# The first layer norm of two row groups taken by features instead of by rows

## The chip, the cores and the metric

The kernel runs on one core of one Trainium2 chip. The metric is the device time of one execution in microseconds (us); it is given as the median of three runs. TensorE (PE) multiplies matrices into PSUM, VectorE (DVE), ScalarE (ACT) and GpSimd (POOL) work elementwise, and SyncE (SP) issues the transfers (DMA). Each engine runs its own instructions strictly in the order of the program, and waits where an operand is not there yet.

## What is computed

```
mod = silu(c) @ w_mod                  # six rows of 448: sa, ca, ga, sb, cb, gb
h = layernorm(x) * (1 + ca) + sa       # x: 2048 rows of 448 features, f32
x = x + ga * attention(h)              # q, k, v from h @ wqkv; 16 heads of 28
h = layernorm(x) * (1 + cb) + sb
x = x + gb * gated_mlp(h)              # gelu, a 2048 x 2048 mix over the rows, a gate
```

`layernorm` takes from each row its mean and divides by the square root of its variance plus 1e-5. The change is in the first of the two norms.

## The kernel before

**Groups and layout.** The 2048 rows are four groups g of 512, each of four tiles of 128 rows. The norm needs mean and variance of a row, so x is loaded with rows on partitions (`load_x`, L179). But the matmuls that follow sum over the features, and so want h turned: `hT[g]` has features on partitions, in four blocks c of 128 (the last one has 64 features, held twice), and 512 rows along the free dimension. Each matrix is split in a high part (rounded to the fast f32r format) and a low part (the rest), and `STEPS` (L27) lists the 11 pairs of parts that are multiplied for one result. The parts of `hT[g]` are read in the order high 0, high 2, high 0, high 2, low 0, low 2, high 1, high 1, low 1, and last block 3 (high and low in one).

**The norm of a group.** `ln_stat` (L276) takes mean and variance of a tile on DVE (bn_stats and bn_aggr); `ln_rs` and `rstd_of` (L99) make the reciprocal root on POOL; `ln_norm` (L288) subtracts and scales on DVE (`xn`, L292), and ACT repeats 64 columns (L300). `ln_transpose` (L104) turns the four tiles with 16 transposes on PE (`tp`, L111) into four PSUM banks; for each block ACT applies 1 + ca and sa (L118, `hfull`) and rounds to the high part (L125), and DVE takes the low part (`sub`, L82). `ln_next(g)` (L542) does that for group g, and the statistics and `ln_norm` of group g + 1 between.

**The order around it.** The schedule is written out by hand; program order is the order on every engine. The loop `for g in range(1, NG)` (L562) has for g = 1 and 2: `v_tile(4g)`, `v_tile(4g + 1)`, `ln_next(g + 1)`, `v_tile(4g + 2)`, `v_tile(4g + 3)`, then two `qk_unit` of group g; for g = 3 two `qk_unit` come first. `v_tile` (L323) is 11 matmuls (`pv`, L317) and a copy by ACT; `qk_unit` (L329) is 11 matmuls (`pq`, L335), the split by ACT (L348) and DVE, and two stores to memory by SP (L354). PSUM has seven banks that go round (`bank`, L161).

**What is woven in.** `load_mod` (L167) loads columns of w_mod, `mod_acc` (L228) sums them on DVE, `mod_split` (L245) splits the sum: the high part (`acc_h`) by ACT, the low part (`acc_l`) by the engine that it is given, POOL for pair 1. `mod_sum` (L256) adds over partitions with two matmuls for each of two parts (`pc`, L260), and `mod_bc` and `mod_col` take the results. For g = 2 the split of pair 1 stands in `ln_next(3)`, and its `mod_sum` behind `v_tile(11)`.

**Transfers.** SP issues nearly all of them, in program order, and they run through one queue. A transfer that waits for its data holds up the ones behind it.

Of the kernel before, what the change touches and what calls it, by code (L numbers as in the profile page):

```python
# [20 lines left out]
NG = 4  # L21
# [9 lines left out]


@with_exitstack
def tile_adaln_mha_gmlp(ctx, tc, x, wqkv, wo, w_in, w_spT, b_sp, w_out, cT, w_mod0, w_mod, out):
    nc = tc.nc
    ctx.enter_context(tc.manual_schedule())
    pe, dve, act, pool, sp = nc.tensor, nc.vector, nc.scalar, nc.gpsimd, nc.sync
# [61 lines left out]
    def rstd_of(var, rs, n):  # L99

        pool.tensor_scalar(out=rs, in0=var, scalar1=EPS, scalar2=None, op0=ALU.add)
        pool.tensor_tensor(out=rs, in0=rs, in1=mhalf[:, :n], op=ALU.pow)

    def ln_transpose(xns, full_pool, dsts, scol, bcol, engs, los=(pool,) * 4, mid=None, after=None):  # L104

        tps = []
        for c in range(4):
            tp = bank("tp")
            tps.append(tp)
            for t in range(4):  # L110
                pe.transpose(tp[:, t * 128 : (t + 1) * 128], xns[t][:, c * 128 : (c + 1) * 128], ident)  # L111
        if mid:
            mid()
        for c in (0, 2, 1, 3):
            tp = tps[c]
            f = full_pool.tile([128, 512], F32, name="hfull")
            if engs[c] is act:
                act.activation(f, tp, AF.Identity, scale=scol[:, c : c + 1], bias=bcol[:, c : c + 1])  # L118
            else:
                engs[c].tensor_scalar(  # L120
                    out=f, in0=tp, scalar1=scol[:, c : c + 1], scalar2=bcol[:, c : c + 1], op0=ALU.mult, op1=ALU.add
                )
            hi = dsts[:, c if c < 3 else 6, :]
            if engs[c] is act:
                act.activation(hi, f, AF.Copy)  # L125
            else:
                engs[c].tensor_copy(hi, f)
            if c < 3:
                sub(los[c], dsts[:, 3 + c, :], f, hi)
            else:  # L130
                sub(los[c], hi[64:128], f[64:128], hi[64:128])
            if after:
                after(c)
# [33 lines left out]
    def load_mod(pair, eng):  # L167
        for k in range(4):
            wms[pair, k] = e1.tile([128, 2 * D], F32, name="wm", tag=("wm", "wm", "raw")[pair], bufs=4)[:, : 2 * D if k < 3 else D]
            c0 = ((pair - 1) * 7 + 2 * k) * D * 128  # L170
            eng.dma_start(wms[pair, k], w_mod[c0 : c0 + (2 if k < 3 else 1) * D * 128].rearrange("(r n) -> r n", r=128))
# [7 lines left out]
    def load_x(g, eng):  # L179
        xg = e1.tile([128, 4, D], F32, name="xg")  # L180
        for t0, t1 in ((0, 1), (1, 2), (2, 4)) if g == 0 else ((0, 4),):
            (act if t1 - t0 == 1 else eng).dma_start(xg[:, t0:t1, :], x[g, :, t0:t1])
        for t in range(4):
            xts[4 * g + t] = xg[:, t, :]
# [43 lines left out]
    def mod_acc(pair, k):  # L228
        if k == 0:
            accs[pair] = e2.tile([128, 2, D], F32, name="acc")  # L230
        wm, acc = wms.pop((pair, k)), accs[pair]
        if k < 3:
            wm = wm.rearrange("r (p n) -> r p n", p=2)
        if k == 0:
            dve.tensor_scalar(out=acc, in0=wm, scalar1=silu[:, 0:1], scalar2=None, op0=ALU.mult)
        elif k < 3:
            dve.scalar_tensor_tensor(out=acc, in0=wm, scalar=silu[:, k : k + 1], in1=acc, op0=ALU.mult, op1=ALU.add)
        else:
            half_rows(wm, [acc[:, part] for part in range(2)])
# [5 lines left out]
    def mod_split(pair, eng, pool_l, tag_l, bufs_l):  # L245

        acc = accs.pop(pair)
        accs[pair] = []
        for part in range(2):
            h = stage.tile([128, 512], F32R, name="acc_h", tag="qf")[:, :D]  # L250
            l = pool_l.tile([128, D], F32R, name="acc_l", tag=tag_l, bufs=bufs_l)
            act.activation(h, acc[:, part, :], AF.Copy)
            sub(eng, l, acc[:, part, :], h)
            accs[pair].append((h, l))
# [21 lines left out]
    def ln_stat(g, ts):  # L276
        if g not in mv1:
            mv1[g] = e1.tile([128, 4, 2], F32, name="mv"), e1.tile([128, 4], F32, name="rs")
        for t in ts:
            st = e1.tile([128, 6], F32, name="st", bufs=4)  # L280
            dve.bn_stats(out=st, in_=xts[4 * g + t])
            dve.bn_aggr(out=mv1[g][0][:, t, :], in_=st)

    def ln_rs(g, a, e):
        mv, rs = mv1[g]
        rstd_of(mv[:, a:e, 1], rs[:, a:e], e - a)

    def ln_norm(g, ts):  # L288
        mv, rs = mv1[g]
        for t in ts:  # L290
            xn = e1.tile([128, 512], F32, name="xn", bufs=4)
            dve.tensor_scalar(  # L292
                out=xn[:, :D],
                in0=xts.pop(4 * g + t),
                scalar1=mv[:, t, 0:1],
                scalar2=rs[:, t : t + 1],
                op0=ALU.subtract,
                op1=ALU.mult,
            )
            act.activation(xn[:, D:], xn[:, 384:D], AF.Copy)  # L300
            xn1.setdefault(g, []).append(xn)
# [21 lines left out]
    def v_tile(kt):  # L323
        v_copy(*v_mm(kt))
# [206 lines left out]
    qk_lo("a", 1, dve)  # L531
    qk_lo("a", 3, dve)
    load_mod(1, sp)
    ln_norm(1, range(4))
    qk_unit((0, 3), 0, order=HI_FIRST)

    def ln_step(g, t):
        ln_stat(g, (t,))
        if t % 2:
            ln_rs(g, t - 1, t + 1)  # L540

    def ln_next(g):  # L542

        if g + 1 < NG:
            ln_transpose(
                xn1.pop(g), e1, hT[g], cols["ca"], cols["sa"], (act,) * 4, (dve,) * 4, None,
                lambda c: ln_step(g + 1, (0, 2, 1, 3).index(c)),
            )
            ln_norm(g + 1, range(4))
        else:  # L550
            ln_transpose(
                xn1.pop(g), e1, hT[g], cols["ca"], cols["sa"], (act,) * 4, (dve,) * 4, None, lambda c: c == 2 and mod_split(1, pool, e1, "wm", 4)
            )

    ln_next(1)
    load_x(3, sp)
    qk_unit((1,), 0)
    qk_unit((2,), 0)
# [3 lines left out]
    for g in range(1, NG):  # L562
        if g == 3:
            early.close()
            stk = att.enter_context(tc.tile_pool(name="stk", bufs=1))
            kq = [[stk.tile([128, S], F32R, name=f"{n}st{i}") for n in "kq"] for i in range(3)]
            kst, qst = [a[0] for a in kq], [a[1] for a in kq]
            npool = att.enter_context(tc.tile_pool(name="npool", bufs=2))
            late_s = ExitStack()
            late_l = late_s.enter_context(tc.tile_pool(name="late_l", bufs=2))  # L570

            def pads(i, eng):

                dve.memset(kst[i][64:128, :].bitcast(F32), 0.0)
                eng.memset(qst[i][64:128, :].bitcast(F32), 0.0)
                pool.memset(kst[i][64:86, :].bitcast(F32), 1.0)

            pads(0, dve)

            def load_head(h, c0=0, c1=S):  # L580
                k, q = kst[h % 3], qst[h % 3]
                if h > 2:
                    sp.dma_start(q[84:86, :].bitcast(F32), q[86:88, :].bitcast(F32))
                for r0, i in ((0, 0), (56, 1), (28, 0)):
                    sp.dma_start(k[r0 : r0 + 28, c0:c1].bitcast(F32), qk_scr[i][D + h * DH : D + (h + 1) * DH, c0:c1])
                for r0, i in ((0, 0), (28, 1), (56, 0)):
                    sp.dma_start(q[r0 : r0 + 28, c0:c1].bitcast(F32), qk_scr[i][h * DH : (h + 1) * DH, c0:c1])

            load_head(0, 0, 1536)
            for m in (0, 3):  # L590
                qk_unit((m,), g)
            load_head(0, 1536, S)
        v_tile(4 * g)
        if g == 3:
            mod_split(2, dve, late_l, "acc_l", 2)
        v_tile(4 * g + 1)
        if g == 3:
            pads(1, pool)
            pads(2, pool)
        if g + 1 < NG:  # L600
            ln_next(g + 1)
        for k in range(2):
            v_tile(4 * g + 2 + k)
            if g == 2 and k == 1:
                mod_bc("ga", 1, 0)
                mod_col("sb", 1, 1, 0.0)
            if g == 1 or g == 2 and k == 1:
                mod_acc(g, k if g == 1 else 0)
        if g < 3:
            for k, m in enumerate((0, 3)):  # L610
                qk_unit((m,), g)
                mod_acc(g, 3 - g + k)
            if g == 2:
                mod_acc(g, 3)
# [887 lines left out]
```

## Time and profile before

| | |
|---|---|
| median of three runs | 1394.73 us (1394.36 to 1395.47) |
| the profiled execution, its own time | 1395.17 us |
| its span, first to last instruction | 1393.4 us |
| instructions | 20303 |
| granted clock of TensorE, mean | 1.000 |
| busy: PE, DVE, ACT, POOL | 1388.3, 1024.4, 779.9, 286.2 us |

The profile is that of one execution. Its views used here are the page (busy times, the chain that ended last), the timeline of one engine (start, length, engine, line, operation, output<-inputs, count, and in brackets the idle time before it and what ended it), the groups by line (busy time and mean in ns, then the idle time before them), the view of one tile or line (shortest, median and longest duration in ns), and the table by stretches (busy time of each engine with the number of instructions, granted clock, DMA share, GB/s). All times are from the start of the span. PE matmuls overlap, so the distance from one start to the next is what one costs.

### The profile page before, as it was taken

The numbers are of one execution on the slowest core, as the hardware profiler recorded it, in microseconds if no ns is written. First come the engines' busy times: TensorE is split into PE (matmuls) and PEld (weight loads), VectorE is DVE, ScalarE is ACT, GpSimd is POOL, SyncE is SP. The second block draws the span as 40 slices with busy tenths as digits, with TensorE's granted clock in tenths as the row PEclk, the third lists the DMA queues.
The fourth block names the chain that finished last, engine by engine and source line by source line (L and its number), as shares of the span: only waits on it lengthen the run. The fifth ranks groups of instructions, "written<-read, shape, count | busy, mean of one in ns | idle before, by whom it ended". The sixth has DMA issues, their size and how long they took to land.

```text
span 1393.4 us, 20303 instructions
## 1 busy us (share of the span) xinstructions
PE 1388.3 (100%) x7170; PEld 988.5 (71%) x7170; DVE 1024.4 (74%) x1742; ACT 779.9 (56%) x1498; POOL 286.2 (21%) x306
## 2 busy tenths in 40 slices
PE   9999999999999999999999999999999999999998
PEld 8888655555555555555555555988998888888888
DVE  7798888888888888888888851850366655668574
ACT  6623677766666777777777779363234544434211
POOL 2144212221224243323200021000142430000000
PEclk9999999999999999999999999999999999999999
DMA  8464644655465556555323002434103333445453
GB/s 285 143 177 173 188 115 151 176 169 156 152 174 162 166 163 185 165 160 155 108 68 78 20 18 72 165 119 140 46 9 105 112 111 110 143 138 164 142 171 113
DMA packets 99489, 187.01 MB, mean 134 GB/s; under 512 B 17656, under 2 KB 29434, under 8 KB 96842
## 3 DMA queue, kind: packets, MB, share of 16 engines
q1 hardware_dynamic: 96670, 181.42, 43.0%
q10 hardware_dynamic: 2718, 4.30, 0.8%
q8 instruction: 56, 0.92, 0.3%
q14 instruction: 45, 0.37, 0.1%
HBM read 130.42 MB, written 50.46 MB: 130 GB/s over the span
## 4 chain that ended last, share of the span: by engine, by line
PE 98%; DMA 1%; DVE 0%; SPq 0%; POOL 0%; issue 0%; ACT 0%
PE st_ps L671 19%; PE o_ps L686 17%; PE mt L639 17%; PE acc L1246 7%; PE acc L1247 7%; PE acc L1248 7%; PE z_ps L1172 5%; PE z_ps L1058 5%; PE pq L335 5%; PE wo_ps L927 3%; PE pv L317 2%; PE y_ps L1353 2%; PE y_ps L1352 2%; PE y_ps L1354 2%; PE tp L111 1%; DMA xg<-in_x_dram 1%
## 5 line engine op out<-in xcount | busy, mean ns | idle before, releaser
L644 DVE TENSOR_REDUCE pm<-mt 128x1 f32<-128x512 f32 x1024 | 631.0, 682 | 85.9 <-PE mt L639 85.8
L675 ACT ACTIVATE P<-st_ps 128x512 f32<-128x512 f32 x1024 | 514.6, 632 | 201.7 <-PE st_ps L671 201.7
L671 PE MATMUL st_ps<-qst,kst 128*128 128x512 f32 x1024 | 404.4, 406 | 0.0
L639 PE MATMUL mt<-kst,qst 128*128 128x512 f32 x1024 | 402.4, 393 | 0.0
L671 PEld LDWEIGHTS st_ps<-qst,kst 128*128 128x128 f32 x1024 | 191.2, 187 | 141.1 <-issue 93.1
L686 PE MATMUL o_ps<-P,V 128*32 128x512 f32 x2048 | 247.1, 598 | 0.0
L639 PEld LDWEIGHTS mt<-kst,qst 128*128 128x128 f32 x1024 | 192.4, 188 | 31.8
L790 POOL TENSOR_TENSOR ws_raw<-ws_raw 128x512 f32<-128x512 f32 x80 | 103.1, 1289 | 293.5 <-DMA ws_raw<-in_w_spT_dram 293.4
L1134 ACT ACTIVATE wsp_h<-raw_sp 128x512 fp32r<-128x512 f32 x112 | 69.9, 631 | 153.5 <-PE acc L1248 104.0
L686 PEld LDWEIGHTS o_ps<-P,V 128*32 128x32 f32 x2048 | 54.6, 109 | 122.9 <-issue 114.6
L82 DVE TENSOR_TENSOR wsp_l<-raw_sp,wsp_h 128x512 fp32r<-128x512 f32 x112 | 80.6, 729 | 82.1 <-ACT wsp_h L1134 81.4
L1246 PE MATMUL acc<-wsp_h,heapA 128*128 128x512 f32 x224 | 87.3, 390 | 0.0
L1247 PE MATMUL acc<-wsp_l,heapA 128*128 128x512 f32 x224 | 87.2, 389 | 0.0
L1248 PE MATMUL acc<-wsp_h,heapA 128*128 128x512 f32 x224 | 87.2, 389 | 0.0
L1247 PE MATMUL acc<-wsp_l,heapB 128*128 128x512 f32 x174 | 67.7, 389 | 0.0
L1248 PE MATMUL acc<-wsp_h,heapB 128*128 128x512 f32 x174 | 67.7, 389 | 0.0
L1246 PE MATMUL acc<-wsp_h,heapB 128*128 128x512 f32 x174 | 67.7, 389 | 0.0
L335 PE MATMUL pq<-heapD,heapD 128*128 128x512 f32 x196 | 61.9, 390 | 0.0
L1176 DVE BATCH_NORM_STATS2 stz<-z 128x6 f32<-128x448 f32 x32 | 19.9, 625 | 50.4 <-ACT z L1175 29.8
L1246 PEld LDWEIGHTS acc<-wsp_h,heapA 128*128 128x128 f32 x224 | 42.1, 188 | 9.0 <-DVE cD L1252 0.3
L1248 PEld LDWEIGHTS acc<-wsp_h,heapA 128*128 128x128 f32 x224 | 42.0, 188 | 8.7
L1247 PEld LDWEIGHTS acc<-wsp_l,heapA 128*128 128x128 f32 x224 | 42.1, 188 | 8.5
(225 smaller groups left out, 1597.5 us busy)
## 6 DMA issues: line engine op xcount, KB each, us to landing
ws_raw<-in_w_spT_dram SPq DMA_DIRECT2D x160, 256.0 KB
ws_scr<-ws_raw SPq DMA_DIRECT2D x80, 256.0 KB
raw_sp<-ws_scr SPq DMA_DIRECT2D x80, 256.0 KB
kst<-qk_scr SPq DMA_DIRECT2D x45, 224.0 KB
qst<-qk_scr SPq DMA_DIRECT2D x45, 224.0 KB
raw_sp<-in_w_spT_dram SPq DMA_DIRECT2D x32, 256.0 KB
qk_scr<-qh SPq DMA_DIRECT2D x28, 256.0 KB
qk_scr<-ql SPq DMA_DIRECT2D x28, 256.0 KB
```

The source lines that it names most:

```text
L82: eng.tensor_tensor(out=dst, in0=a, in1=hi.bitcast(F32), op=ALU.subtract)
L335: pe.matmul(pq, wqk[:, b, m * 128 : (m + 1) * 128], hT[g][:, a, :], start=j == 0, stop=j == NST - 1)
L639: pe.matmul(mt, qst[h % 3][:, t * 128 : (t + 1) * 128], kst[h % 3][:, kb * 512 : (kb + 1) * 512], start=True, stop=True)
L644: dve.tensor_reduce(out=pms[h][:, t, kb : kb + 1], in_=mt, axis=AX.X, op=ALU.max)
L671: pe.matmul(st, kst[h % 3][:, kt * 128 : (kt + 1) * 128], qst[h % 3][:, qb * 512 : (qb + 1) * 512], start=True, stop=True)
L675: act.activation(p, st, AF.Exp, scale=SCALE)
L686: pe.matmul(otile[h][32 * qb : 32 * qb + 32, :], V[:, kt, h, :], ptiles.pop((u, qb)), start=kt == 0, stop=kt == NT - 1)
L790: pool.tensor_tensor(out=a, in0=a, in1=b, op=SUMS[i // 16][2])
L1134: act.activation(hi, raw, AF.Copy)
L1246: pe.matmul(acc[i], zh, hi, start=st == 0, stop=False)
L1247: pe.matmul(acc[i], zh, lo, start=False, stop=False)
L1248: pe.matmul(acc[i], zl, hi, start=False, stop=st == 7)
```

## The change

Groups 0 and 1 stay. For groups 2 and 3, x is also laid out turned in memory (`xT`: per group four blocks of 128 features by 512 rows, the last one's 64 features twice), and is loaded in that form (`load_xT`). The statistics are taken from x with rows on partitions as before. `ln_rows` makes of them, per row, the factor (reciprocal root) and the addend (minus mean times root), stores both as two lines of 512 in memory, each as 512 single elements, and loads each line back onto all 128 partitions (`abr`). `ln_rank` multiplies a block by the one and adds the other, in place, two tensor_tensor on DVE or POOL; `ln_fin` does the rest (1 + ca and sa on ACT, high part on ACT, low part on DVE). The transposes, `xn` and the PSUM banks of these groups are gone. Group 3's rows are loaded (`load_x(3)`) after the stores and loads of group 2's two lines.

```diff
+    ln_stat(2, (0,))
     ln_norm(1, range(4))
     qk_unit((0, 3), 0, order=HI_FIRST)
...
+    def load_xT(g):
+        for c in (0, 2, 1, 3):
+            xcs[g, c] = e1.tile([128, 512], F32, name="xc", tag="xn", bufs=4)
+            sp.dma_start(xcs[g, c], xT[g - 2, c])
+
+    def ln_rows(g):
+
+        mv, rs = mv1[g]
+        rstd_of(mv[:, :, 1], rs, 4)
+        ab = e1.tile([128, 2, 4], F32, name="ab")
+        pool.tensor_copy(ab[:, 0, :], rs)
+        dve.scalar_tensor_tensor(out=ab[:, 1, :], in0=mv[:, :, 0], scalar=-1.0, in1=rs, op0=ALU.mult, op1=ALU.mult)
+        dst = scr.tile([2, 512], F32, name=f"ab_scr{g}")
+        for i in range(2):
+            sp.dma_start(dst[i].rearrange("(t p) -> p t", p=128), ab[:, i, :])
+        abs_[g] = []
+        for i in range(2):
+            t = e1.tile([128, 512], F32, name="abr", tag="hfull")
+            sp.dma_start(t, dst[i].rearrange("(o n) -> o n", o=1).broadcast_to([128, 512]))
+            abs_[g].append(t)
+
+    def ln_rank(g, c, eng):
+        for t, op in zip(abs_[g], (ALU.mult, ALU.add)):
+            eng.tensor_tensor(out=xcs[g, c], in0=xcs[g, c], in1=t, op=op)
+
+    def ln_fin(g, c):
+        xc, hi = xcs.pop((g, c)), hT[g][:, c if c < 3 else 6, :]
+        act.activation(xc, xc, AF.Identity, scale=cols["ca"][:, c : c + 1], bias=cols["sa"][:, c : c + 1])
+        act.activation(hi, xc, AF.Copy)
+        if c < 3:
+            sub(dve, hT[g][:, 3 + c, :], xc, hi)
+        else:
+            sub(dve, hi[64:128], xc[64:128], hi[64:128])
 
     def ln_next(g):
 
-        if g + 1 < NG:
-            ln_transpose(
-                xn1.pop(g), e1, hT[g], cols["ca"], cols["sa"], (act,) * 4, (dve,) * 4, None,
-                lambda c: ln_step(g + 1, (0, 2, 1, 3).index(c)),
-            )
-            ln_norm(g + 1, range(4))
-        else:
-            ln_transpose(
-                xn1.pop(g), e1, hT[g], cols["ca"], cols["sa"], (act,) * 4, (dve,) * 4, None, lambda c: c == 2 and mod_split(1, pool, e1, "wm", 4)
-            )
+        ln_transpose(
+            xn1.pop(g), e1, hT[g], cols["ca"], cols["sa"], (act,) * 4, (dve,) * 4, None,
+            lambda c: c != 3 and ln_stat(2, ((0, 2, 1).index(c) + 1,)),
+        )
 
     ln_next(1)
+    load_xT(2)
+    ln_rows(2)
     load_x(3, sp)
...
-        if g + 1 < NG:
-            ln_next(g + 1)
-        for k in range(2):
-            v_tile(4 * g + 2 + k)
-            if g == 2 and k == 1:
+        if g < 3:
+            for c, eng in ((0, dve), (1, dve), (2, pool), (3, pool)) if g == 1 else ((1, dve), (0, pool), (2, pool), (3, pool)):
+                ln_rank(g + 1, c, eng)
+        if g == 1:
+            ln_fin(2, 0)
+            ln_stat(3, (0, 1))
+            v_tile(6)
+            ln_fin(2, 1)
+            ln_stat(3, (2,))
+            mod_acc(1, 0)
+            v_tile(7)
+            ln_fin(2, 2)
+            ln_stat(3, (3,))
+            ln_fin(2, 3)
+            load_xT(3)
+            ln_rows(3)
+            mod_acc(1, 1)
+        else:
+            v_tile(4 * g + 2)
+            if g == 2:
+                ln_fin(3, 1)
+                mod_split(1, pool, e1, "wm", 4)
+            v_tile(4 * g + 3)
+            if g == 2:
+                ln_fin(3, 0)
                 mod_bc("ga", 1, 0)
                 mod_col("sb", 1, 1, 0.0)
-            if g == 1 or g == 2 and k == 1:
-                mod_acc(g, k if g == 1 else 0)
+                mod_acc(2, 0)
         if g < 3:
             for k, m in enumerate((0, 3)):
                 qk_unit((m,), g)
+                if g == 2:
+                    ln_fin(3, 2 + k)
                 mod_acc(g, 3 - g + k)
```

More of the change, by code (lines that the diff above doesn't have):

```diff
@@ L33, in tile_adaln_mha_gmlp @@
 @with_exitstack
-def tile_adaln_mha_gmlp(ctx, tc, x, wqkv, wo, w_in, w_spT, b_sp, w_out, cT, w_mod0, w_mod, out):
+def tile_adaln_mha_gmlp(ctx, tc, x, xT, wqkv, wo, w_in, w_spT, b_sp, w_out, cT, w_mod0, w_mod, out):
     nc = tc.nc
@@ L533, in tile_adaln_mha_gmlp @@
     load_mod(1, sp)
+    ln_stat(2, (0,))
     ln_norm(1, range(4))
     qk_unit((0, 3), 0, order=HI_FIRST)
[L537 to L540, printed above, removed]
-    def ln_next(g):
-        if g + 1 < NG:
-            ln_transpose(
-                xn1.pop(g), e1, hT[g], cols["ca"], cols["sa"], (act,) * 4, (dve,) * 4, None,
-                lambda c: ln_step(g + 1, (0, 2, 1, 3).index(c)),
-            )
-            ln_norm(g + 1, range(4))
-        else:
-            ln_transpose(
-                xn1.pop(g), e1, hT[g], cols["ca"], cols["sa"], (act,) * 4, (dve,) * 4, None, lambda c: c == 2 and mod_split(1, pool, e1, "wm", 4)
-            )
+    xcs, abs_ = {}, {}
@@ L1462 @@
     cT[:64, 3] = cT[64:, 4] = _np.asarray(inputs["c"]).reshape(448)[384:]
+    xt = _np.asarray(inputs["A_x"])[0].T
     wm = _np.asarray(inputs["w_mod"]).reshape(448, 3, 2, 448)
@@ L1479 @@
         "x": _np.asarray(inputs["A_x"])[0].reshape(4, 4, 128, 448).transpose(0, 2, 1, 3),
+        "xT": _np.stack([xt[:128], xt[128:256], xt[256:384], _np.concatenate([xt[384:], xt[384:]])])
+        .reshape(4, 128, 4, 512)
+        .transpose(2, 0, 1, 3)[2:],
         "wqkv": twice(inputs["A_wqkv"]),
```

## The prediction, made before the changed kernel was run

> **What bounds the kernel now.** I read the page's busy table and its chain first, then TensorE's own chain for the stretch the change touches (30 to 75 us), then each other engine's timeline there.
>
> ```profile
> PE 1388.3 (100%) x7170; PEld 988.5 (71%) x7170; DVE 1024.4 (74%) x1742; ACT 779.9 (56%) x1498; POOL 286.2 (21%) x306
> PE 98%; DMA 1%; DVE 0%; SPq 0%; POOL 0%; issue 0%; ACT 0%
> ```
>
> TensorE (PE) is the bound: it is busy throughout and is 98% of the chain. So removed PE time is gained in full, and any wait put on PE is lost in full. The chain of the stretch, in order of time (start, length, what):
>
> ```profile
> 30.26 5.01 PE pq L335 x22
> 35.27 4.48 PE pv L317 x22
> 39.76 1.75 PE tp L111 x16
> 41.51 4.69 PE pv L317 x22
> 46.19 5.04 PE pq L335 x22
> 51.23 4.48 PE pv L317 x22
> 55.71 1.75 PE tp L111 x16
> 57.46 4.49 PE pv L317 x22
> 61.95 0.81 PE pc L260 x4
> 62.76 9.99 PE pq L335 x44
> ```
>
> No gap: `v_tile` (pv) costs 2.24 us each, a `qk_unit` (pq) 2.5 us, the four `mod_sum` matmuls (pc) 0.81 us. The two `tp` rows are what the change removes; the first unit of g = 3, which reads hT[3], starts two units after 62.76, at 67.8.
>
> **What goes.** The transposes of groups 2 and 3: 2 x 1.75 = **3.5 us** off PE. DVE loses eight `xn` and ACT eight 64-column copies; neither is late today, so this is worth nothing by itself.
>
> **What comes in their place** is a serial chain per group: statistics, reciprocal root on POOL, a store of two 512-element rows in 4-byte pieces, two loads that spread them over 128 partitions, two tensor_tensor per block, two ACT passes, one subtraction. I follow it with these prices.
>
> ```profile
> 24.48 0.18 DVE L282 BATCH_NORM_AGGREGATE mv<-st 128x2 f32<-128x6 f32 x1
> 35.13 0.18 DVE L282 BATCH_NORM_AGGREGATE mv<-st 128x2 f32<-128x6 f32 x1
> 24.75 0.59 POOL L101 TENSOR_SCALAR rs<-mv 128x4 f32<-128x4 f32 x1 [0.54 <-DVE mv L282]
> 25.42 1.33 POOL L102 TENSOR_TENSOR rs<-rs,mhalf 128x4 f32<-128x4 f32 x1
> 64.48 0.29 SPq L269 DMA_DIRECT2D sb_scr<-row  x1
> 65.63 1.63 SPq L272 DMA_DIRECT2D col_sb<-sb_scr  x3
> 66.50:68.30 1.80, 1.80 (x10) 1.49 (x9) 1.19 (x2) 0.50 (x1) 0.00 (x0) 1.00 0.14 1
> 3.51 0.63 DVE L281 BATCH_NORM_STATS2 st<-xg 128x6 f32<-128x448 f32 x1 [2.37 <-DMA xg<-in_x_dram]
> L182 ACTq DMA_DIRECT2D xg<-in_x_dram x2: 413/436/458, 0.7 to 1.2; - x2
> 31.45 0.45 SPq L182 DMA_DIRECT2D xg<-in_x_dram  x1
> L654 POOL CAST mxp<-mxv 128x16 fp32r<-128x16 f32 x16 | 3.1, 196 | 1.1
> 40.80:50.40 9.60, 9.60 (x49) 8.27 (x48) 8.21 (x18) 7.48 (x14) 1.45 (x3) 1.00 0.84 277
> ```
>
> (The two rows that begin with a stretch, 66.50:68.30 and 40.80:50.40, end with the granted clock, the DMA share and GB/s.)
>
> Group 2. One of its four statistics moves ahead of `ln_norm(1)`, into DVE's idle time before the `xn` of group 1; so the last is aggregated in the slot of the 35.13 row, 35.3. From aggregate to root is 24.66 to 26.75, 2.1 us for four columns: 37.4; POOL's copy, some 0.3 with the gap (0.2 for 16 columns): 37.7. A store's round trip is 64.48 to 65.63, 1.15 us for one 1.8 KB piece. No row has 512 four-byte pieces written; the nearest has as many read (`col_sb`, done inside the 1.8 us of the row 66.50:68.30 at a share of 0.14). Bounds 1.2 and 4 us; I take 2, near the read. A load of 224 KB takes 0.7 to 3.5, 2.8 us with others beside it. SP waits for each store before it issues the load: 39.6 and 40.3. The rows are thus in place at about **42.3 and 43.0**. On SP, `load_xT(2)`, four issues, goes ahead of all this and costs nothing (no other transfer is due), but `load_x(3)`, issued at 31.45 before, now stands behind both stores and loads, at some 41; its data arrive at 45, before the 47.8 at which DVE asks for them.
>
> Next, the blocks of group 2. Prices:
>
> ```profile
> L715 POOL TENSOR_TENSOR osb<-osb,rb 128x512 f32<-128x512 f32 x15 | 19.2, 1280 | 134.1 <-DMA rb<-r_scr 130.8 <-DVE pm L644 3.3
> L118 ACT ACTIVATE hfull<-tp,col_sa,col_ca 128x512 f32<-128x512 f32 x12 | 9.2, 769 | 0.0
> L125 ACT ACTIVATE heapD<-hfull 128x512 fp32r<-128x512 f32 x12 | 7.6, 633 | 0.4
> 59.00 0.69 DVE L82 TENSOR_TENSOR heapD<-hfull,heapD 128x512 fp32r<-128x512 f32 x1 [0.63 <-ACT heapD L125]
> 59.51 2.34 POOL L82 TENSOR_TENSOR acc_l<-acc,acc_h 128x448 fp32r<-128x448 f32 x2 [7.95 <-ACT acc_h L252]
> 61.26 1.14 DVE L82 TENSOR_TENSOR heapD<-hfull,heapD 128x512 fp32r<-128x512 f32 x1 [1.57 <-ACT heapD L125]
> 1055.03 1.28 DVE L82 TENSOR_TENSOR wsp_l<-raw_sp,wsp_h 128x512 fp32r<-128x512 f32 x2
> 1055.25 5.12 POOL L1140 TENSOR_TENSOR z<-z,z 128x384 f32<-128x384 f32 x2 [1.89 <-DVE z L1185]
> ```
>
> The DVE row at 61.26 matters: the same subtraction as at 59.00 takes 1.14 instead of 0.69, and ends 0.55 after POOL's `acc_l` (61.85). And POOL's two adds at 1055.25 took 5.12 while DVE ran subtractions. So a DVE operation with two SBUF inputs and a POOL tensor_tensor **take turns**. The change puts four ranks' operations on DVE and four on POOL at the same moment. With turns (DVE 0.6, POOL 1.28 each): block 0 is ranked at 44.8, block 1 and block 2 at about 47, block 3 at 50.2. ACT (0.77 + 0.63 a block, V copies between) and DVE (subtractions, statistics of group 3, `mod_acc`) then finish block 0's low part at 47.8, block 1's at 50.8, block 2's at 52.9, block 3's at 54.2; the last statistic of group 3, queued on DVE behind block 2, ends at 53.6.
>
> PE, without transposes, wants `v_tile(8)` at 51.23 - 1.75 = 49.5, block 2's low part six matmuls of 0.2 in, block 3 at the tenth: it waits some 3 us. `v_tile` 8 to 11 end at about 61.4 instead of 61.95: nearly all the gain is spent here.
>
> **The wait that decides** is at the four `mod_sum` matmuls behind `v_tile(11)`. They read `acc_l`, which POOL makes in `mod_split(1)`. Before, POOL was empty (7.95 us idle) and had it at 61.85. After, `mod_split` stands in POOL's program order **behind six ranks of group 3**. These need the spread rows of group 3: statistics 53.6, root 55.7, copy 56.0, stores at 56.0 and 56.4. The one queue has by then to move, from 41.8 on, x of group 3 (0.9 MB), four q/k stores (1.0), `load_mod(2)` (1.6) and xT of group 3 (1.0): 4.6 MB, which at 277 GB/s (the row 40.80:50.40) end at 58.5; there the stores came in late and singly, here they are issued together, so I take 57. Store landed 58.4, rows in place **61.1 and 61.8**. POOL then runs 6 x 1.28 = 7.7 us, gives way to DVE's two ranks and two subtractions (4 x 0.6 = 2.4): 71.2. Two `acc_l` of 1.17: 72.4, 73.5. PE stands from 61.4 to 72.4 and again for the second `acc_l`; `qk_unit(0, 2)` starts at 73.6 instead of 62.76: **+10.8**, with the 3.5 gained already inside. Behind PE's wait everything of ACT and DVE that follows (`bc_ga`, `row`, the q/k evictions) waits as well. DVE has a wait of its own, in `ln_rows(3)` for the root, 54.2 to 55.7; `mod_acc(1, 1)` to `(1, 3)` and two q/k subtractions stand behind it, are done by 61, and PE needs none of them earlier (their banks come round again after `v_tile(11)`).
>
> Two smaller terms. `ln_fin(3, 3)` stands behind the eviction of `qk_unit(3, 2)`: 0.6 + 0.77 + 0.63 + 0.69 and latencies, 2.9 us after that unit ends, while the first unit of g = 3 reads block 3 at its tenth matmul, 9 x 0.2265 = 2.0 in: **+0.9**. And the clock: this kernel's PE never stands a microsecond in the middle, so the trace does not show what a stand of 11 us does. It shows the start:
>
> ```profile
> L224 PE MATMUL wu<-ones x30: 275/421/582, 1.0 to 7.3; 128*128 128x128 f32 x30
> L224 PE MATMUL wu<-ones,xg x2: 275/275/275, 10.2 to 10.3; 128*128 128x128 f32 x2
> ```
>
> The same shape has a median of 421 ns in the first 6.3 us and 275 later (the granted clock prints 1.00 in both, the durations don't agree with it): 30 in 6.3 us against 0.11 us apart later, 3 us lost. Bounds 0 and 3.2; I take **+2.5**, near the only row. The Trainium skill (TensorE: Matmul & The Clock Gate, Part 1) has the clock halved after an idle window of some 3.4 us and restored after a busy one; by it the stand would cost an estimated 1.7 to 3.4 us, and without it the sum would be 2.5 lower.
>
> Sum: 10.8 + 0.9 + 2.5 = 14.2 on the profiled execution's 1395.17 (span 1393.4): 1409.4; the median shown is 0.44 lower, so **1409.0 us**. From 75 us on PE is the bound again and nothing gives time back.
>
> **Rivals.**
> - *All waits covered* (faster). If the rows of group 3 were in place by 49, POOL's 7.7 + 2.3 us would be done before PE needs `acc_l` at 58.5 and only the 3.5 would count: 1391.2. Against it: DVE asks for group 3's last statistic behind block 2's subtraction, and even with no turns, stores of 1.2 us and an empty queue the rows of group 2 come at 41.5, ACT needs 5 us for blocks 0 to 2 with two V copies between (47.4), the last statistic ends at 48.8, and root, copy, store and load add 5.4: 54.2. Chance 0.03.
> - *The clock stays*: same waits, 1406.5. The granted clock of 1.00 in every row speaks for it, the start's durations against. Chance 0.22.
> - *No turns, quick queue*: POOL's six run in 7.7 us from 59.5 on, `acc_l` done at 70: +7.5 + 0.9, at the clock's cost or none, 1400 to 1405. For it: ranks in place have dependent steps between which the other engine could slip. Chance 0.16.
> - *Four-byte writes are slow*: each store 4 us or more, so both chains shift, 1411 to 1416. The Trainium skill (DMA: Bandwidth & Descriptors, Specifications) says that a transfer under 512 B is a read-modify-write; no row here has one written, and it gives no price. Chance 0.12.
> - *It doesn't do what it says*: `acc_l` gets past the ranks on POOL after all. Then the wait moves to block 3 of hT[3], which is ranked at 71 and ready at 73 where PE wants it at 69: still +3.5, 1398. Chance 0.02.
>
> **Numbers.** The forecast has 0.45. Best ends of every term (rows of group 3 at 54.2 to 56.5, no turns, no clock loss) give some +4.5, 1399; worst ends 1415. Range 1399 to 1415, leaving out the first rival and the far end of the slow writes. About 0.2% (2.8 us) is what a measurement of this kernel can tell from no change: slower 0.93, within 0.03, faster 0.04.
>
> **What will show it.** PE's waits: `pc` L260 on POOL `acc_l`, about 10 us, near 61; `pv` on DVE `heapD`, about 3 us, near 50; a short wait of `pq` on `heapD`. POOL: its first rank of group 3 at about 61, of group 2 at about 42; ranks and DVE's tensor_tensor longer than 1.28 and 0.69. For a few microseconds after the stand pq matmuls are longer than now:
>
> ```profile
> L335 PE MATMUL pq<-heapD,heapD 128*128 128x512 f32 x131 | 42.0, 390 | 0.0
> ```
>
> It is wrong if POOL's rank operations of group 3 begin before 50, if no row has PE waiting on POOL, or if the time from `v_tile(11)` to the first `mt` is the old one.

## The result, and the profile after

The changed kernel takes 1431.17 us (median of six runs, 1430.42 to 1432.11); the kernel before took 1395.07 beside it. The ratio is 1.0258, with a 95% interval of 1.0245 to 1.0271: **36 us slower**, where 14 were forecast and 1415 was the upper end of the range. Each experiment below has a ratio to runs of the kernel before on its own chip, and those ratios are what is compared.

The page's chain (TensorE was 98% of it) now reads:

```profile
PE 93%; ACT 0%; DVE 0%; issue 0%
```

The missing time is TensorE standing. The waits of its weight loads between 20 and 130 us, without two below 0.5 us (output, engine and tile waited for, sum, how often, longest):

```profile
PEld pc L260 <- ACT acc_h L252: 14.0, 1, 14.0
PEld pv L317 <- ACT heapD L568: 13.2, 2, 8.3
PEld pc L260 <- POOL acc_l L82: 6.3, 2, 5.7
PEld pv L317 <- DVE heapD L82: 1.3, 2, 1.1
PEld pq L335 <- DVE heapD L82: 1.2, 1, 1.2
```

That is 36.0 us, at the three places that the forecast named: `v_tile(8)` (`pv`, 14.5 instead of 3), `mod_sum` (`pc`, 20.3), and block 3 of hT[3] (`pq`, 1.2). (The 3.5 us of transposes that are gone and the halved clock behind the stands nearly cancel.) Why so much? SP's own timeline shows the stores of the two lines (L554) and the loads that wait for them (L558):

```profile
38.10 0.94 SPq L554 DMA_DIRECT2D ab_scr<-ab  x2
47.46 1.09 SPq L558 DMA_DIRECT2D abr<-ab_scr  x2
...
68.14 0.93 SPq L554 DMA_DIRECT2D ab_scr<-ab  x2
80.16 0.81 SPq L558 DMA_DIRECT2D abr<-ab_scr  x2
```

From a store's issue to the load's it is 9.4 us for group 2 and 12.0 for group 3, for 4 KB. The table by stretches shows what the DMA engines did meanwhile, and what clock TensorE was granted (the last three columns are clock, DMA share and GB/s):

```profile
41.00:43.00 2.00, 2.00 (x11) 1.84 (x11) 0.09 (x1) 0.00 (x0) 0.00 (x0) 1.00 0.00 0
43.00:45.00 2.00, 2.00 (x12) 1.82 (x11) 0.00 (x0) 0.00 (x0) 0.00 (x0) 1.00 0.00 0
...
54.60:68.30 13.70, 5.67 (x13) 4.07 (x14) 12.01 (x18) 7.81 (x13) 7.83 (x7) 0.50 0.84 295
...
78.50:99.10 20.60, 5.35 (x12) 3.61 (x13) 7.03 (x7) 4.14 (x7) 11.20 (x8) 0.50 0.25 76
```

The first two rows say that the DMA engines were idle and nothing moved, while ACT, POOL, the queue and, but for 0.09 us, DVE stood, and the loads still waited for the stores. The last two are the two stretches with the halved clock. POOL, then ACT, then TensorE at the wait that decides:

```profile
53.86 6.78 POOL L563 TENSOR_TENSOR xc<-xc,abr 128x512 f32<-128x512 f32 x4 [15.79 <-issue]
84.12 9.23 POOL L563 TENSOR_TENSOR xc<-xc,abr 128x512 f32<-128x512 f32 x6 [16.01 <-issue]
93.32 2.24 POOL L82 TENSOR_TENSOR acc_l<-acc,acc_h 128x448 fp32r<-128x448 f32 x2
```

```profile
86.49 0.81 ACT L567 ACTIVATE xc<-xc,col_sa,col_ca 128x512 f32<-128x512 f32 x1 [13.32 <-DVE xc L563]
...
87.87 1.03 ACT L252 ACTIVATE acc_h<-acc 128x448 fp32r<-128x448 f32 x2
```

```profile
88.48 0.74 PE L260 MATMUL pc<-acc_h,ones_r 128*128 128x448 f32 x1 [13.66 <-ACT acc_h L252]
94.50 0.74 PE L260 MATMUL pc<-acc_l,ones_r 128*128 128x448 f32 x1 [5.27 <-POOL acc_l L82]
...
96.15 1.48 PE L335 MATMUL pq<-heapD,heapD 128*128 128x512 f32 x3
```

The six ranks, then `acc_l`, then TensorE: the order is the forecast's, 23 us later. The forecast left out `acc_h`: ACT makes it behind a block of group 3, so TensorE stood for it first (14.0 us) and for `acc_l` after that (6.3). `acc_l` came last and set the end. `qk_unit(0, 2)` starts at 96.15 instead of 62.76.

### The profile page after: what moved, and what is told of

The parts are those of the page before. It is cut to its first block, busy times and chain, and to the rows that moved or that the text cites. A ratio compares the mean times of both kernels' runs of the same rounds, so it can differ in the third digit from the quotient of the medians.

```text
span 1428.6 us, 20271 instructions
## 1 busy us (share of the span) xinstructions
PE 1391.0 (97%) x7138; PEld 987.3 (69%) x7138; DVE 1030.3 (72%) x1742; ACT 778.4 (54%) x1490; POOL 301.0 (21%) x314
## 4 chain that ended last, share of the span: by engine, by line
PE 93%; ACT 0%; DVE 0%; issue 0%
PE st_ps L720 18%; PE o_ps L735 17%; PE mt L688 17%; PE acc L1295 6%; PE acc L1297 6%; PE acc L1296 6%; PE z_ps L1221 5%; PE z_ps L1107 5%; PE pq L335 4%; PE wo_ps L976 3%; PE y_ps L1402 2%; PE y_ps L1403 2%; PE y_ps L1401 2%; PE pv L317 1%; PE tp L111 1%; PE mtp L709 0%
```

## The experiments

My theory after the result: **the stores are what was mis-sized**; 512 pieces of 4 bytes, neighbours in memory, take some 10 us, twice in the one chain, and the rest of the chain stands as forecast. Rivals: the number of pieces; the wait for the store (not the store); POOL's turns and order; DVE's extra work.

### What a store of small pieces costs

`p_forms` is the kernel before with seven small stores behind its last load, each followed by a read of one element of what it wrote. The pieces are views of one memory tile:

```diff
+    by4 = lambda d: d.rearrange("(t p) -> p t", p=128)
+    for k in range(2):
+        d4 = form(f"p4_{k}", [512], by4, mhalf, one)
+    form("p16", [512], lambda d: d.rearrange("(p t) -> p t", t=4), mhalf, one)
+    form("p4far", [512, 16], lambda d: by4(d[:, 0]), mhalf, lambda d: d[0:1, 0:1])
+    form("p4apart", [512, 128], lambda d: by4(d[:, 0]), mhalf, lambda d: d[0:1, 0:1])
+    form("p512", [4, 128], lambda d: d, ident[0:4, :], lambda d: d[0:1, 0:1])
+    form("p4one", [128], by4, mhalf[:, 0:1], one)
```

> The kernel before, and behind its last load seven small stores to memory on SP, each followed by a read of one stored element, which SP can issue only when the store is complete: so the distance from the issue of a store to the issue of its read is the store's round trip. Forms: 512 pieces of 4 bytes into one line of 2 KB (twice), 128 pieces of 16 bytes, 512 pieces of 4 bytes 64 bytes apart, the same 512 bytes apart, 4 rows of 512 bytes, 128 pieces of 4 bytes; last the load of the line onto 128 partitions. Theory (completion): the completion of many small writes is what costs, 5 us or more for 512 adjacent pieces, 2 us or less for 16-byte pieces, 1.2 us for rows; if neighbours in one line get in each other's way, the pieces 64 or 512 bytes apart take under 3 us, if the number of pieces counts alone, they take as long as the adjacent ones. Rival (queue): the store waited for other transfers in the changed kernel; then every form takes 1 to 2 us here, where nothing else is in the queue.

SP's timeline; the distance from a store (L1464) to its read (L1460) is the price:

```profile
1376.14 0.43 SPq L1464 DMA_DIRECT2D p<-mhalf  x1
1386.06 0.25 SPq L1460 DMA_DIRECT2D probe<-p  x1
...
1397.44 0.33 SPq L1464 DMA_DIRECT2D p<-mhalf  x1
1398.85 0.23 SPq L1460 DMA_DIRECT2D probe<-p  x1
1399.13 0.36 SPq L1464 DMA_DIRECT2D p4far<-mhalf  x1
1402.26 0.23 SPq L1460 DMA_DIRECT2D probe<-p4far  x1
1402.54 0.36 SPq L1464 DMA_DIRECT2D p4apart<-mhalf  x1
1404.30 0.23 SPq L1460 DMA_DIRECT2D probe<-p4apart  x1
...
1406.01 0.35 SPq L1464 DMA_DIRECT2D p4one<-mhalf  x1
1414.18 0.22 SPq L1460 DMA_DIRECT2D probe<-p4one  x1
```

512 neighbours of 4 bytes: 9.9 us (10.8 the second time). The same 512 pieces 64 bytes apart: 3.1; 512 bytes apart: 1.8. The same bytes in 128 pieces of 16: 1.4; in rows of 512 bytes 1.2. And only 128 neighbours of 4 bytes: 8.2. The kernel's last output stores (224 KB each) still ran beside the two stores of 512 neighbours and beside the one 64 bytes apart; the other four had nothing beside them. So it is not the number of pieces (512 at 1.8, 128 at 8.2). Nor is it that they lie side by side alone, for pieces of 16 bytes side by side take 1.4: slow are pieces of 4 bytes that are neighbours. Why, no run here shows. The Trainium skill (DMA: Bandwidth & Descriptors, Specifications) has a transfer under 512 B as a read-modify-write; the direction agrees, but size alone does not set the price here: pieces of 4 bytes at 1.8 us, when they are far apart, are as far under 512 B as those at 9.9.

### The same store in pieces of 16 bytes

`e1_pieces16` changes one view, so that factors and addends reach other rows than their own; `e6_own_rows` also loads x of groups 2 and 3 so that a partition holds four rows that stand together, as that view wants it.

```diff
-            sp.dma_start(dst[i].rearrange("(t p) -> p t", p=128), ab[:, i, :])
+            sp.dma_start(dst[i].rearrange("(p t) -> p t", t=4), ab[:, i, :])
```

> The changed kernel with the two lines stored in another order of the rows, so that each partition writes one piece of 16 bytes (128 pieces a line instead of 512); means and roots so reach other rows than their own, the work is the same. Theory (completion, by the number of pieces): the stores of group 2, 9.4 us from issue to the loads' issue, and of group 3, 12.0 us, fall to 3 us or so each; both lie on the same chain, so 1431 falls by some 15 us to 1416. Rival (POOL): the time is lost by the ranks on POOL and their turns with VectorE; then 1431 stays within 3 us.

> The change, with x of groups 2 and 3 laid out so that a partition holds four rows that stand together; the powers and means then go out as 128 pieces of 16 bytes, in the right order. Theory (what the price of the store added was the neighbouring 4-byte pieces, nothing else): as the kernel with 16-byte pieces in the wrong order, 1413.6, so 1411 to 1416. Rival (the order of the pieces or the layout of x mattered): over 1418.

1413.61 us, ratio 1.0131 (1.0102 to 1.0160), and 1412.88, ratio 1.0129 (1.0114 to 1.0145). Stores and loads of e6:

```profile
38.11 0.80 SPq L554 DMA_DIRECT2D ab_scr<-ab  x2
41.51 0.80 SPq L558 DMA_DIRECT2D abr<-ab_scr  x2
...
60.42 0.80 SPq L554 DMA_DIRECT2D ab_scr<-ab  x2
61.86 0.79 SPq L558 DMA_DIRECT2D abr<-ab_scr  x2
```

3.4 and 1.4 us where the change has 9.4 and 12.0, and half of the loss is gone: 1.0258 - 1.0129 is 18 us. With stores at the price that the forecast had taken (2 us), the time is 18 us above before, not 14. By the trace the loads have the largest share in the other 4, though no run isolates it: the first ranks of e6 start 3.6 us (group 2) and 4.9 us (group 3) after the loads were issued, where I had 2.8.

### Is it the wait, or the store?

`e4_no_wait` loads the two lines from `b_sp`, so that no load waits for a store. `e5_rows` turns `ab` with one small transpose and stores it as rows of 512 bytes.

```diff
-            sp.dma_start(t, dst[i].rearrange("(o n) -> o n", o=1).broadcast_to([128, 512]))
+            sp.dma_start(t, b_sp[i * 512 : (i + 1) * 512].rearrange("(o n) -> o n", o=1).broadcast_to([128, 512]))
```

```diff
+        pe.transpose(tp[0:8, 0:128], abs_[g].rearrange("p a b -> p (a b)"), ident)
...
+        act.activation(abt, tp[0:8, 0:128], AF.Copy)
...
-        for i in range(2):
-            sp.dma_start(dst[i].rearrange("(t p) -> p t", p=128), ab[:, i, :])
+        sp.dma_start(dst.rearrange("i (t p) -> (i t) p", p=128), abt)
```

> The changed kernel, in which the lines are spread over the partitions from an input (b_sp) instead of from the line just stored; the stores are still issued in their place, but no load waits for them. The normalised values are wrong by that, the work is the same. Theory (completion): the loads are issued at 39 instead of 47.5, the ranks of group 2 begin at 42 instead of 54, those of group 3 at some 60 instead of 84; what is left is the forecast's own sum, 1405 to 1410. Rival (POOL): 1425 or more. Rival (broadcast load: 128 reads of one line are slow): the ranks still begin 6.5 us after the loads' issue, and 1412 to 1418 is left.

> The changed kernel with factor and addend turned by one small transpose on TensorE (8 columns) and stored as 8 rows of 512 bytes; for that the store stands behind v_tile(4) and v_tile(8), and load_mod(2) behind the first. Theory (completion): round trip 1.2 to 1.6 us instead of 9.4 and 12.0; 1403 to 1410, with the wait for the second acc_l on POOL still the largest. Rival (POOL): 1425 or more. No theory has it below 1395, because POOL's six ranks still stand ahead of acc_l.

Both missed. e4: 1425.81, ratio 1.0218 (1.0189 to 1.0248): taking the wait away brought only 6 us. By its number this is the rival that blames POOL (1425 or more); the 18 us of e6, which leaves POOL as it is, speak against that. Its group 3 loads are issued at once, at 65.54, and its first rank starts at 78.90. The stretches between show why:

```profile
66.00:68.00 2.00, 2.00 (x8) 1.80 (x7) 2.00 (x4) 0.00 (x0) 0.00 (x0) 0.58 0.13 1
68.00:70.00 2.00, 2.00 (x11) 1.83 (x10) 0.99 (x2) 0.55 (x1) 0.00 (x0) 1.00 0.17 8
```

With 0.5 MB of loads outstanding the engines move 1 and 8 GB/s. The stores hold up what comes behind them, waited for or not. e5: 1417.81, ratio 1.0161 (1.0131 to 1.0190), no faster than e6: its stores take 3.8 us for group 2 (40.05 to 43.81) and 2.4 for group 3 (65.76 to 68.19), and group 3's stand behind a tile of V and a copy by ACT and leave at 65.76 instead of e6's 60.42.

### One queue, or all?

`e10_other_queue` is e4 with the stores issued by ACT. `p_queue` measures it behind the last load of the kernel before: one load of 128 rows of 1792 bytes by SP (L1473), and a small transfer that waits for it (L1474), alone and behind a store (L1480 on SP, or on ACT). The comments in the second diff are not in the kernel.

```diff
-            sp.dma_start(dst[i].rearrange("(t p) -> p t", p=128), ab[:, i, :])
+            act.dma_start(dst[i].rearrange("(t p) -> p t", p=128), ab[:, i, :])
```

```diff
+    load(0)
+    case(1, sp, by4)     # the load behind 512 x 4 B in the same queue
+    case(2, act, by4)    # behind 512 x 4 B that ACT issues
+    case(3, sp, by16)    # behind 128 x 16 B in the same queue
```

> As the kernel that loads its rows without waiting for the stores (the rows it uses are 1024 numbers of b_sp, so every block of groups 2 and 3 is wrong in its values, and the same in its work; it stood at 1425.8), but the 4-byte stores are issued by ACT instead of SP, into a queue of their own. Theory (the outstanding writes hold up what is queued behind them): SP's loads land 3 to 6 us after their issue as with pieces of 16 bytes, and the time falls to 1407 to 1413. Rival (the writes hold up every transfer, whichever queue it is in): 1421 or more, and the engines move as little in those stretches as before.

> The kernel before, with work put behind its end (so its time means nothing): one load of 128 rows of 1792 bytes by SP, from its issue to the issue of a small transfer that waits for it, four times: alone; just behind a store of 512 pieces of 4 bytes, neighbours in memory, in the same queue; just behind such a store that ACT issues; and behind a store of 128 pieces of 16 bytes in the same queue. Theory (writes of neighbours occupy the engines, whichever queue they are in): about 2.5 us alone, 6 or more behind the 4-byte store in either queue, and 3 to 4 behind the 16-byte one. Rival (only the queue's own order holds it up): 6 or more behind the 4-byte store in SP's own queue, and 2.5 to 3.5 with the store in ACT's.

e10 fell between the two: 1418.25, ratio 1.0160 (1.0146 to 1.0174). Its group 2 loads went out at 34.97, ahead of the stores at 37.92, and were held little (the first rank on POOL starts at 39.26, the next at 42.73); its group 3 loads, issued two microseconds behind ACT's stores, were held 10 us:

```profile
58.91 0.94 SPq L558 DMA_DIRECT2D abr<-in_b_sp_dram  x2
```

```profile
69.33 9.23 POOL L563 TENSOR_TENSOR xc<-xc,abr 128x512 f32<-128x512 f32 x6 [12.55 <-DMA abr<-in_b_sp_dram]
```

p_queue settles it (SP's timeline):

```profile
1376.66 0.43 SPq L1473 DMA_DIRECT2D pline<-in_x_dram  x1
1379.47 0.25 SPq L1474 DMA_DIRECT2D tiny<-pline  x1
...
1382.33 0.34 SPq L1473 DMA_DIRECT2D pline<-in_x_dram  x1
1393.93 0.24 SPq L1474 DMA_DIRECT2D tiny<-pline  x1
...
1396.47 0.36 SPq L1473 DMA_DIRECT2D pline<-in_x_dram  x1
1407.99 0.22 SPq L1474 DMA_DIRECT2D tiny<-pline  x1
...
1411.04 0.33 SPq L1473 DMA_DIRECT2D pline<-in_x_dram  x1
1415.97 0.24 SPq L1474 DMA_DIRECT2D tiny<-pline  x1
```

Alone the load takes 2.8 us; behind the 4-byte store 11.6; with that store in another engine's queue 11.5; behind the 16-byte store 4.9 (I had expected 3 to 4). The kernel's last output stores, which ACT issued until 1391.9, ran beside the first two loads; beside the third there was only the small store, so its 11.5 is not their doing. The rival (only the queue's order) fell: another queue doesn't help. The Trainium skill (DMA: Bandwidth & Descriptors, Issuing engines are not separate DMA queues) says that transfers run on the same engines whoever starts them; these two numbers agree. Which part between the DMA engines and the memory is occupied, no run here shows.

### POOL: its order and its turns

On e6, `e7_own_split` puts `mod_split(1)`, that is `acc_h` on ACT and `acc_l` on POOL, ahead of group 3's ranks, and `e8_own_split_dve` also gives all ranks to DVE.

```diff
+        if g == 2:
+            mod_split(1, pool, e1, "wm", 4)
         if g < 3:
-            for c, eng in ((0, dve), (1, dve), (2, pool), (3, pool)) if g == 1 else ((1, dve), (0, pool), (2, pool), (3, pool)):
+            for c, eng in ((0, dve), (1, dve), (2, dve), (3, dve)) if g == 1 else ((1, dve), (0, dve), (2, dve), (3, dve)):
```

> As e6, and the split of the modulation sums (acc_h by ACT, acc_l by POOL) stands ahead of group 3's six ranks on POOL instead of behind them. Theory (TensorE waited for acc_l because it was queued behind the ranks): the waits of pc for acc_h (3.0 us) and acc_l (5.6) go, the last block of hT[3] becomes the wait, at about 79 us, inside qk_unit(0,3), which would have ended at 89 before: 7 us less, 1406 to 1408. Rival (the ranks are late for all that stands behind, so the wait only moves): 1412 or more.

> As e7, with all ranks on DVE, none on POOL. Theory (POOL and DVE take turns: 1.55 us a rank on POOL, 0.69 on DVE alone): group 3's eight ranks take 5.5 us on DVE instead of 9.3 beside POOL, hT[3] is whole at about 74 and no wait is left there; 1400 to 1404. Rival (DVE then holds up the subtractions behind the ranks, and group 2 loses what group 3 gains): 1406 or more.

e7: 1406.67, ratio 1.0080 (1.0063 to 1.0097), as the theory had it: the split behind the ranks cost 7 us. Of e6's waits for it, 6.5 us were for `acc_l` and 3.4 for `acc_h`; this run moves both and doesn't tell them apart. The waits of `pq` grew from 1.2 to 4.5 us.

```profile
67.36 2.30 POOL L82 TENSOR_TENSOR acc_l<-acc,acc_h 128x448 fp32r<-128x448 f32 x2 [4.55 <-ACT acc_h L252]
69.62 9.73 POOL L563 TENSOR_TENSOR xc<-xc,abr 128x512 f32<-128x512 f32 x6
```

e8: 1404.82, ratio 1.0075 (1.0060 to 1.0090), not to be told from e7 and above its 1400 to 1404. Eight ranks on DVE do take only 5.8 us (POOL needs 9.7 for six), but DVE's subtractions stand behind all eight, and the wait of `pq` on them is 3.7 us (3.2 in e7). The time fell between theory and rival (1406 or more); the hold-up that the rival named for group 3 is there.

### Can the chain be hidden?

`e9_reorder` writes the order anew: group 2's statistics ahead of group 1's blocks and group 3's right behind them, so that group 2's store could go at 35 us instead of 38, the subtractions between the ranks, `mod_acc` and `mod_split` ahead of group 3. `e11_own_queue` is e9 with the lines stored and loaded by ACT, group 3's store a little later. `e12_all_early` is e9 with x(3) loaded behind group 2's lines, group 3's statistics therefore behind group 2's blocks, and the sums of both pairs moved to where DVE waits for the rows. The comments in the diff are not in the kernels.

```diff
+    load_x(3, sp)                       # e9; in e12 behind ln_get(2)
     ln_norm(1, range(4))
+    ln_stat(2, (1,))
     qk_unit((0, 3), 0, order=HI_FIRST)
+    ln_stat(2, (2, 3))
...
-            sp.dma_start(dst[i].rearrange("(p t) -> p t", t=4), ab[:, i, :])
+            act.dma_start(dst[i].rearrange("(p t) -> p t", t=4), ab[:, i, :])      # e11
...
+    mod_acc(1, 0)                       # e12: all of pair 1 here, pair 2 behind qk_unit(0, 1)
+    mod_acc(1, 1)
```

> As e8, and the order written anew: the statistics of groups 2 and 3 before the blocks of group 1 are finished, the rows of group 2 stored at about 35 us instead of 38, x(3) loaded before q and k are stored, the low parts of the second half of wqk on POOL, the subtractions between the ranks, the modulation sums ahead of group 3. Theory (the change lost nothing but cover: rows at 40 us, blocks of group 2 done at 48, before TensorE wants them at 49.7, group 3's at 59 before 63.5): all waits covered, the transposes' 3.5 us gained, 1391 to 1394. Rival (the queue, at its full rate from 23 to 40 us, brings the rows later than that): 1396 to 1402.

> As e9, with the stores and loads of the rows issued by ACT, so that they are not behind x(3), q, k and the turned x in SP's queue. Theory (in e9 it was the queue: 37.75 to 43.26 us from store to load, 3.7 more to the first rank): the rows of group 2 land at about 42 instead of 47, the 3.9 us of waits in v_tile(8) go, and the wait of 3.8 for the memsets of kst with them, since group 3 comes earlier as well; 1391 to 1394.5, at or below the kernel before. Rival (the 16 engines are shared, and full until 44 us, whichever queue it is): 1398 or more.

> As e9 (rows in SP's queue, 16-byte pieces, all ranks on DVE), with x(3) loaded behind group 2's rows instead of ahead of them, and the modulation sums of both pairs, 4.2 us of DVE each, taken out of the stretch behind the ranks: pair 1 while DVE waits for group 2's rows (37 to 42 us), pair 2 while it waits for group 3's. Theory (what e9 has left is two things: rows that come 4 to 5 us late behind 0.9 MB of x(3), 3.9 us of waits in v_tile(8), and a DVE without a gap from 47 to 83 us, so that kst is cleared late, 3.8 us): both go, 1391 to 1395, level with the kernel before or a little below. Rival (DVE cannot carry 16 ranks of 0.7 us beside its other work in this stretch, wherever they stand, or the small pieces are slow under load whatever is queued ahead): 1397 or more.

All three missed: 1401.31, ratio 1.0044 (1.0029 to 1.0059); 1403.15, 1.0055 (1.0041 to 1.0069); 1403.96, 1.0055 (1.0042 to 1.0069). In e9 the store could leave only at 37.75, behind x(3), the turned x, and q and k that were still being stored, and under that load the small pieces took 5.5 us:

```profile
37.75 1.58 SPq L555 DMA_DIRECT2D ab_scr<-ab  x2
43.26 1.04 SPq L561 DMA_DIRECT2D abr<-ab_scr  x2
```

In e11, with a queue of their own, they took as long (35.06 to 40.99): here too another queue didn't help. In e12 the store left at 35.18, as soon as the last of the rows was computed (35.15), and yet the second operand of the first rank was there only at 47:

```profile
35.18 0.80 SPq L554 DMA_DIRECT2D ab_scr<-ab  x2
39.13 2.67 SPq L560 DMA_DIRECT2D abr<-ab_scr  x2
```

```profile
47.02 3.35 DVE L565 TENSOR_TENSOR xc<-xc,abr 128x512 f32<-128x512 f32 x5 [2.17 <-DMA abr<-ab_scr]
```

So either the trip through memory (12 us here) or DVE's 16 ranks (11 us) keeps the gain away.

### The same ranks without the trip

`e13_rows_by_pe` is e12 with the ranks left on DVE and the trip taken away: TensorE spreads the rows, by transposing a column that is read 128 times over, and the ranks read them from PSUM. Besides, pair 2's sums stand behind group 3's ranks again. `e14_rows_later` puts these transposes for group 3 one tile of V later.

```diff
-            t = e1.tile([128, 512], F32, name="abr", tag="hfull")
-            sp.dma_start(t, dsts[g][i].rearrange("(o n) -> o n", o=1).broadcast_to([128, 512]))
...
+            tp = bank("abr")
+            for t in range(4):
+                pe.transpose(tp[:, t * 128 : (t + 1) * 128], dsts[g][:, i, t : t + 1].broadcast_to([128, 128]), ident)
...
         if g == 2:
+            v_tile(10)                  # e14
             ln_get(3)
```

> The order of e12, but the rows of powers and means don't go through memory: TensorE spreads them, four transposes of a column read 128 times over for each row, 8 of 128 by 128 for each group (about 1.0 us at 0.12 each) where before has 16; the 16 ranks on DVE stay, and read the rows from PSUM. x of groups 2 and 3 lies as in before; pair 2's modulation sums stand behind group 3's ranks. Theory (the trip through memory, 35 to 47 us from the last statistic to the first sum in e12, is the cost that is left): the waits of TensorE in v_tile(8) and qk_unit(0,3) go, 1392 to 1396. Rival (DVE cannot carry the 16 ranks, 11 us, beside its other work in this stretch): waits of 4 us or more stay, 1399 or more.

> As e13, with the eight transposes that spread group 3's rows one tile of V later, so that TensorE doesn't stand for the last statistics. Theory (what is left of the change is half of its transposes, 16 of 32, and one wait of 2.2): the wait goes, 1394 to 1396, 0.0 to 0.2% below the kernel before. Rival (the wait only moves behind group 3's ranks, to qk_unit(0,3)): as e13, 1396 to 1398.

e13: 1397.26, ratio 1.0007 (0.9998 to 1.0017): level with the kernel before. Of the two that e12 had left open it was the trip (the place of pair 2's sums changed with it, and its part is not isolated); DVE carries the ranks. TensorE's timeline has what the spreading costs, and the one wait of note:

```profile
37.91 1.04 PE L559 MATMUL abr<-ident,ab 128*128 128x128 f32 x8
...
57.07 1.09 PE L559 MATMUL abr<-ident,ab 128*128 128x128 f32 x8 [1.82 <-POOL ab L550]
```

and its waits between 20 and 130 us, that one and the next:

```profile
PEld abr L559 <- POOL ab L550: 2.2, 1, 2.2
PEld mt L690 <- issue: 0.6, 1, 0.6
```

3.5 us of transposes are gone, 2.1 come in, and 2.8 of waits: 1.4 above, and the spans differ by 1.1 (1394.5 against 1393.4). e14: 1398.07, ratio 1.0021 (1.0012 to 1.0030). The wait of 2.2 went from there, but the attention starts no sooner. This profiled execution runs 1.1 us later than e13's already before the edit (group 2's ranks at 45.08 against 44.00); against that, group 3's ranks come 0.2 us later and the first matmul of the attention 0.2 us later. TensorE gets there sooner and stands for a load of q, which came no earlier:

```profile
84.92 0.47 PE L692 MATMUL mt<-kst,qst 128*128 128x512 f32 x1 [2.41 <-DMA qst<-qk_scr]
```

The rival was right that the wait moves, though not where to. By their intervals e14 and e13 can't be told apart. No version here is faster than the kernel before.

## Why the prediction was wrong

The mechanism and the sign were right, a size was not. By its own steps:

| step | forecast | measured |
|---|---|---|
| group 2's store leaves | 37.7 | 38.1 |
| a store's trip | 2 (1.2 to 4) | **9.4, 12.0** |
| a load, to the first rank | 2.8 | 6.4, 3.9 |
| first rank of group 2 | 42.3 | 53.9 |
| waits in `v_tile(8)` | 3 | 14.5 |
| group 3's store leaves | 56.0 | 68.1 |
| first rank of group 3 | 61.1 | 84.1 |
| POOL's six ranks | 7.7 + 2.4 | 9.2 |
| `qk_unit(0, 2)` starts | 73.6 | 96.15 |
| wait for block 3 | 0.9 | 1.2 |
| halved clock after the stand | 2.5 | 2.3 |

- **The step that failed**: "Bounds 1.2 and 4 us; I take 2, near the read." No row had small pieces written, and a read of as many pieces is no bound for a write of them. They took 7.4 and 10 us more, and since group 3's chain starts only behind group 2's blocks, both come in: the first rank of group 3 is 23.0 late, made of 17.4 in the stores and 4.7 in the loads. Against e6, the stores' form alone is 18 us.
- The rival "four-byte writes are slow" had the right cause at the wrong price, 4 us. It also had the pieces' size alone as the reason; 4-byte pieces that are far apart took 1.8 us.
- **The load** was priced from a load of rows at 2.8. It took 3.9 to 6.4 us, and 3.6 to 4.9 in e6, where it is the largest part of what the stores leave of the miss.
- **The order on POOL** was right: the split behind the ranks cost 7 us by e7. But "They read `acc_l`" left out `acc_h`, which stood behind ACT's block of group 3 and held TensorE first. The turns were right, too: a rank's median on POOL is 1592 ns beside DVE, against 1280 in the rows of before, and the six took 9.2, between 7.7 and 10.1.
- **The clock**: the rival "the clock stays" fell. It is granted at 0.50 from 54.6 and from 78.5 us, 4.7 and 3.7 us after TensorE had stopped, and at 1.00 again 5.4 and 4.6 us after it had gone on (from 62.88 and 94.50); 4.6 us at half speed are 2.3 lost, where 2.5 stood. The Trainium skill's rule (TensorE: Matmul & The Clock Gate, Part 1), a halved clock after some 3.4 us of idleness, agrees with these stands.
- The sum: 33.4 to the start of `qk_unit(0, 2)`, and 2.4 in the four units behind it (12.4 us from 96.15 on, where 9.99 stood before), 1.5 of them the half speed until 99.1 and most of the rest block 3: 35.8. The profiled spans differ by 35.2, the medians by 36.1.
- The 3.5 us for the transposes could not be kept: e13 keeps 1.4 of them, and gives that back in waits.

## What to carry to other kernels

Where a transposition by the matrix engine is replaced by a trip through memory, price the trip from issue to first use in the very pattern that is written, with the queue as it stands; from the store's issue to the first rank it took 16 us in 4-byte pieces, and 6 to 12 in pieces of 16 bytes, against 1.75 us of transposes a group. If no row shows the pattern, the range must be as wide as the cover: ask how late the result may come before anything waits, and treat every pattern not seen as later than that. And when a wait is late on an engine with its own order (POOL here), look first at what stands behind it that others need: moving the split was worth 7 us and took no added work.

## What the runs showed of the hardware

- Stores of 4-byte pieces that lie side by side: 8.2 us for 128 of them with nothing else moving, 9.9 and 10.8 for 512 with an output store beside them. 512 pieces 512 bytes apart took 1.8, 128 pieces of 16 bytes side by side 1.4, with nothing else moving; 512 pieces 64 bytes apart took 3.1, with an output store beside them. Beside other traffic the 16-byte pieces took 1.4 to 5.9 us.
- A load that is issued behind such a store lands late, whether the store is in its own queue or in another: one of 2.8 us took 11.6 and 11.5.
- A transpose whose input is one column read 128 times over spreads that column over all partitions; eight of 128 by 128 took 1.04 us.
